# Reordering the first loads, transposes and copies of a fused convolution and two-layer MLP kernel

## The chip, the cores and the metric

The kernel runs on one core of a Trainium2 chip. The metric is device time in microseconds (us) for one execution. One profiled execution of each kernel gives the trace; other executions give a time and a mean granted TensorE clock (the share of its full clock that TensorE was allowed, 1 is full).

PE is TensorE, PEld its weight loads, ACT is ScalarE, DVE is VectorE, POOL is GpSimd, SP is SyncE. L837 means line 837 of that kernel's source.

## The reference, cut to what matters

```python
# x (8, 4096, 192), weight (8 heads, 7 taps): a causal convolution per head, softmaxed taps
w = softmax(weight, axis=-1)
out = np.einsum('hk,bskhg->bshg', w, windows_of(x))      # 6 zeros ahead of each sequence
# then 32768 tokens through w_in (192, 2048) and w_out (2048, 192)
h = out.reshape(-1, 192) @ w_in
g = np.where(h > 0, h, exp(min(h, 0)) - 1)                # ELU
return g @ w_out                                          # float32
```

## The kernel before

Tokens are worked off in 32 "supers" of 1024. In a super there are 16 blocks of 128 hidden columns, and in a block two units (one for each half of the tokens). So there are 1024 units. One unit goes through four engines:

- PE: three matmuls `H <- att, w_in` (64 rows, 512 columns) into one PSUM bank;
- ACT: `E <- exp(H)`;
- POOL: `E <- min(E, 1)`;
- DVE: `gT <- max(E - 1, H)`, after which the PSUM bank is free. I count units by these gT operations.

PE then multiplies gT by w_out into accumulator banks. The convolution of super 0 is done in a special way, so that work can begin early: x is cast, transposed on PE and convolved by matmuls with diagonal tap matrices (a tap is one of the 7 weights of the filter). The halo, `xh` and `xbh` in the code, is the 8 rows of x just before the second half of the tokens; it is cast and transposed apart. The convolutions of later supers take four groups of matmuls with a banded matrix `Tm`; ACT evicts each group (`csb`), and one transposing DMA makes `att` of it. For super 1 these groups stand at the blocks of `EARLY_CONV`.

All of w_in sits twice in SBUF, in partitions 0 to 63 for one unit of a block and 64 to 127 for the other. It is loaded to the lower half through POOL's DMA queue in three parts (blocks 0 to 3, 4 to 7, 8 to 15). The upper half is a copy: parts 0 and 1 by DVE, the third by a DMA that SP issues once it has landed. The parts that the change and the argument touch:

```python
WARM, FILL = (6, 1, 4), 1
WCOLS = ((0, 4 * FC), (4 * FC, 8 * FC), (8 * FC, 16 * FC))
EARLY_CONV = (6, 7, 9, 10)
# ...
start_up = [("t", j) for j in (3, 0, 1, 2)] + [("d", j) for j in range(3)]   # 3: halo
for what in start_up:
    pe_order.append(what)
    if what[0] == "t" and what[1] < 3:
        pe_order.append(("w", 0, FILL))          # a zero matmul, 128x512
# ... POOL: one queue, in this order
load_w_in(0); load_w_in(1); load_w_out(0)        # w_out(0): blocks 0 to 7
load_x(1, 0); load_x(1, 1)
load_w_in(2); load_w_out(1)
load_x(2, 0); load_x(2, 1)
# ... ACT at the start
W(s_xh, 16); activation(xbh <- xh, Copy)         # halo cast
W(s_xs, 16)
for j in range(3): activation(xb[j] <- xs[j], Copy)
# ... SP
# band matrix out to DRAM, wait, Tm back in; then
W(s_w[2], 48)
sy.dma_start(w_in[HP:P, :, c0:c1], w_in[0:HP, :, c0:c1]).then_inc(s_wd, 16)
# ... PE, first matmul of a unit in block q, upper half (r == 1)
W(s_w[part], 48)
if r == 1 and part < 2: W(s_wc, part + 1)
elif r == 1:            W(s_wd, 16)
```

Of the kernel before, what the change touches and what calls it, by code (L numbers as in the profile page):

```python
# [6 lines left out]
ACT = mybir.ActivationFunctionType  # L7
# [28 lines left out]
CONV_AT = (14, 18, 23, 25)  # L36
QB = 2
WARM = (6, 1, 4)
FILL = 1
WCOLS = ((0, 4 * FC), (4 * FC, 8 * FC), (8 * FC, 16 * FC))  # L40
HALO = 8
BW = P + CW
XI = SUP // P
# [3 lines left out]
E_DVE = ()  # L47
HELD = {"h": 2900.0, "c": 1300.0, "a": 1400.0}

EARLY_CONV = (6, 7, 9, 10)  # L50
EARLY_O = (4, 8)
PACE0, UNTIL = 1160.0, 24
X_AT = ((2, 1, 1), (1, 1, 0))
# [3 lines left out]
def bass_lightweight_conv__then__act_elu_kernel(  # L57
# [15 lines left out]
    NQ = FF // FC  # L73
# [12 lines left out]
    pe_order, plan = [], []  # L86
# [100 lines left out]
    for s in range(1, NS):  # L187
        for u in range(CU):
            at = NQ * (s - 2) + CONV_AT[u] if s > 1 else EARLY_CONV[u]
            conv_steps.setdefault(at, []).append(CU * s + u)  # L190


    start_up = [("t", j) for j in (3, 0, 1, 2)] + [("d", j) for j in range(3)]
    for i, (b, what) in enumerate(
        ((0, ("t", 0)), (3, ("t", 3)), (1, ("t", 1)), (2, ("t", 2)))
        + ((4, ("d", 0)), (5, ("d", 1)), (6, ("d", 2)), (7, ("d", 2)))
# [19 lines left out]
    for second in range(2):  # L216
        for rt in range(2):
            g = rt ^ second
            k, b = divmod(NP - O_AT[g], NB)
# [17 lines left out]
    pe_order += [("w", 0, WARM[0]), ("s",), ("w", 0, WARM[2])]  # L237
    for what in start_up:
        pe_order.append(what)
        if what[0] == "t" and what[1] < 3:  # L240
            pe_order.append(("w", 0, FILL))
    pe_order += [item for _, item in sorted(plan, key=lambda p: p[0])]
    turn_at = {}
    dve_order, evacs, unit_at_conv = [], [], {}
    for at, item in sorted(plan, key=lambda p: p[0]):
# [8 lines left out]
        elif item[0] == "o" and item[-1]:  # L254
            turn_at[item[1:3]] = turn_at.get(item[1:3], 0) + 1
            if turn_at[item[1:3]] == visits[item[1:3]]:
                what = ("e",) + item[1:3]
# [25 lines left out]
    with ExitStack() as stack:  # L283
# [6 lines left out]
        def sema(name):  # L290
            return stack.enter_context(nc.semaphore(name))
# [8 lines left out]
        xh = sbuf("xh", [HALO, D], FP32)  # L300
        xbh = sbuf("xbh", [HALO, 3, 2, HP], BF16)
# [22 lines left out]
        H = psum("H", [P, NBANK, GS])  # L324

        s_wq = sema("s_wq")
        s_w = [sema(f"s_w{i}") for i in range(5)]
        s_wc = sema("s_wc")
        s_sel = sema("s_sel")
        s_set = sema("s_set")  # L330
# [5 lines left out]
        s_xh = sema("s_xh")  # L336
        s_wb = sema("s_wb")
        s_xz = sema("s_xz")
        s_cast = sema("s_cast")
        s_tap = sema("s_tap")  # L340
# [47 lines left out]
        def att_need(s):  # L388
# [1 line left out]


        first_read = {
            ("t", 0): (0, 2),
            ("t", 1): (1, 0),
            ("t", 2): (2, 0),
            ("t", 3): (0, 1),
            ("d", 0): (3, 0),
            ("d", 1): (0, 3),
            ("d", 2): (4, 4),
# [69 lines left out]
        @block.gpsimd  # L469
        def _gpsimd(g: bass.BassGpSimd):  # L470
            W = Waits(g)

            def load_x(s, gr):
                b = s % NXB
                if s >= NXB:
                    W(s_cv, CU * (s - NXB))
                if s == NXB:
                    W(s_zw, 1)
                def windows(w0, w1, rows):
                    src = bass.AP(  # L480
                        tensor=x_flat.tensor,
                        offset=(s * SUP + gr * GS + w0 * CW - PAD) * D,
                        ap=[[D, rows], [CW * D, w1 - w0], [1, D]],
                    )
                    g.dma_start(  # L485
                        xg[0:rows, b, 2 * w0 + gr : 2 * w1 : 2, :], src
                    ).then_inc(s_x[b][gr], 16)

                if s == NS - 1 and gr == 1:
                    windows(0, NWIN - 1, P)  # L490
                    windows(NWIN - 1, NWIN, GS - CW * (NWIN - 1) + PAD)
                else:
                    windows(0, NWIN, P)

            def batch_zeros(s):

                W(s_x[s % NXB][0], x_need[s, 0])
                g.memset(xg[0:PAD, s % NXB, 0, :], 0.0).then_inc(s_z)

            def load_w_in(k):  # L500
                c0, c1 = WCOLS[k]
                for j in range(3):
                    g.dma_start(  # L503
                        w_in[0:HP, j, c0:c1],
                        bass.AP(
                            tensor=moe_w_in.tensor,
                            offset=8 * j * FF + c0,
                            ap=[[CPH * FF, HEADS], [FF, 8], [1, c1 - c0]],
                        ),
                    ).then_inc(s_w[k], 16)  # L510

            def load_w_out(k):
                q = slice(NQ // 2 * k, NQ // 2 * (k + 1))
                g.dma_start(
                    w_out[:, q, :], moe_w_out.rearrange("(q p) d -> p q d", p=FC)[:, q, :]
                ).then_inc(s_w[3 + k], 16)

            g.memset(ones[:], 1.0).then_inc(s_id)
            W(s_id, 1)
            g.affine_select(  # L520
                out=ident[:],
                in_=ones[:],
                pattern=[[-1, P]],
                compare_op=ALU.is_equal,
                fill=0.0,
                base=0,
                channel_multiplier=1,
            ).then_inc(s_id)
            for step in range(2):
                W(s_id, 2 + step)  # L530
                g.affine_select(
                    out=owner[:, :],
                    in_=owner[:, :] if step else ones[0:HEADS, :],
                    pattern=[[0, 2], [1 - 2 * step, HP]],
                    compare_op=ALU.is_ge,
                    fill=0.0,
                    base=7 * step,
                    channel_multiplier=8 * (2 * step - 1),
                ).then_inc(s_id)
            W(s_id, 4)  # L540
            g.affine_select(
                out=block8[:, :, :],
                in_=ones[0:HEADS, 0 : HEADS * KSIZE].rearrange("p (h k) -> p h k", h=HEADS),
                pattern=[[1, HEADS], [0, KSIZE]],
                compare_op=ALU.is_equal,
                fill=0.0,
                base=0,
                channel_multiplier=-1,
            ).then_inc(s_id)
            load_w_in(0)  # L550
            load_w_in(1)
            load_w_out(0)
            for gr in range(2):
                load_x(1, gr)
            load_w_in(2)
            load_w_out(1)
            for gr in range(2):
                load_x(2, gr)
            for i, (n, u) in enumerate(units):
                s, at_n = divmod(i // 2, NQ)  # L560
                if i % 2 == 0 and at_n == ZERO_AT and (s + 2) % SPB == 0 and s + 2 < NS:
                    batch_zeros(s + 2)
                for to_load in x_before.get(i, ()):
                    load_x(*to_load)
                W(s_exp, i + 1)
                g.tensor_scalar(  # L566
                    out=E[:, i % NE, :],
                    in0=E[:, i % NE, :],
                    scalar1=1.0,
                    scalar2=0.0,  # L570
                    op0=ALU.min,
                    op1=ALU.max,
                ).then_inc(s_clp)

        @block.scalar
        def _scalar(a):
            W = Waits(a)
# [5 lines left out]
            a.activation(scr[:, 1:2], scr[:, 0:1], ACT.Exp)  # L583
            W(s_set, 2)
            a.activation(wex[:], wq2[:], ACT.Exp).then_inc(s_wex)
            W(s_xh, 16)
            a.activation(  # L587
                xbh[:, :, 1, :].rearrange("p j (h e) -> p j h e", e=8),
                xh[:, :].rearrange("p (h j e) -> p j h e", j=3, e=8),
                ACT.Copy,  # L590
            ).then_inc(s_cast)
            W(s_xs, 16)
            for j in range(3):
                a.activation(  # L594
# [12 lines left out]
            for item in act_order:  # L607
# [4 lines left out]
                elif item[0] == "h":  # L612
                    i = unit_at[item[1:]]
# [10 lines left out]
        def _vector(v):  # L624
            W = Waits(v)

            def upper_half(v, k):
                c0, c1 = WCOLS[k]
                W(s_w[k], 48)
                v.tensor_copy(w_in[HP:P, :, c0:c1], w_in[0:HP, :, c0:c1]).then_inc(s_wc)  # L630
# [39 lines left out]
                H[:, bank_of["d", 2], 0:KSIZE].unsqueeze(2).to_broadcast([P, KSIZE, P]),  # L670
                ALU.mult,
            ).then_inc(s_tap)
            v.tensor_copy(
                wband[:, :, P - KSIZE : P][:, :, ::-1],
                H[:, bank_of["d", 2], HP : HP + HEADS * KSIZE].rearrange(
                    "p (h k) -> p h k", h=HEADS
                ),
            ).then_inc(s_tap)
            for at, j in enumerate((3, 0)):
                W(s_xt, at + 1)  # L680
                v.tensor_copy(*transposed(j)).then_inc(s_fd)
            upper_half(v, 0)
            W(s_first, 2)
            v.tensor_copy(*first_att(1, 0, GS)).then_inc(s_fd)  # L684
            W(s_first, 3)
            v.tensor_copy(*first_att(2, GS // 2, GS)).then_inc(s_fd)
            upper_half(v, 1)
            for item in dve_order:
                if item[0] == "e":
                    v.tensor_copy(*out_evac(W, *item[1:])).then_inc(s_od)  # L690
# [2 lines left out]
                i = unit_at[n, u]  # L693
                s, q = divmod(n, NQ)
# [14 lines left out]
        def _tensor(pe):  # L709
            W = Waits(pe)  # L710
# [15 lines left out]
            for item in pe_order:  # L726
# [25 lines left out]
                elif item[0] == "t":  # L752
                    j = item[1]
                    W(s_id, 2)
                    if j < 3:
                        W(s_cast, j + 2)
                        for i in range(XI):
                            for g in range(2):
                                rows = slice(HP * g, HP * (g + 1))
# [6 lines left out]
                                    tile_position=(HP * g, HP * g),  # L766
                                )
                    else:
                        W(s_xz, 1)
                        W(s_cast, 1)  # L770
                        for jj in range(3):
                            ins = pe.matmul(
                                H[:, bank_of[item], HALO * jj : HALO * (jj + 1)],
# [5 lines left out]
                    ins.then_inc(s_xt)  # L779
                elif item[0] == "d":  # L780
                    j = item[1]
                    W(s_tap, 2)
                    first_evacuated(W, ("t", j))
                    first_evacuated(W, ("t", 3))
                    for tap in range(KSIZE):
# [61 lines left out]
                else:  # L847
# [6 lines left out]
                        wait_bank(("a", k, g))  # L854
                    if visit is not None and not opens:
                        W(s_turn[g], turns[k, g])
                    W(s_w[3 + q // (NQ // 2)], 16)
                    W(s_tt, tt_count(NQ * t + q, g))
                    t0 = 2 * P * half + P * kb
                    ins = pe.matmul(  # L860
# [80 lines left out]
```

## Time and profile before

| What | Value |
|---|---|
| time, first three runs | 730.87 us median (730.77 to 732.73) |
| span of the profiled run | 730.1 us (its time 732.09 us, mean granted clock 0.994) |
| PE busy | 721.1 us, 99% |
| period of 32 units once it runs evenly (units 128 to 1000) | 21.87 us |
| gT unit 0 / 16 / 36 starts | 16.09 / 29.09 / 43.70 us |

From the page of the profiled run, the busy table's row of all engines and the row of the granted clock (40 slices of 18 us, 9 is full):

```profile
PE 721.1 (99%) x11856; PEld 682.7 (93%) x11857; DVE 640.7 (88%) x1042; ACT 677.3 (93%) x1287; POOL 669.2 (92%) x1114
...
PEclk9899999999999999999999999999999999999999
```

PE is full nearly everywhere; only the second slice has a clock below full. The change can only matter at the start. Here is the chain of waits of the kernel before (start, duration, what), around 24 us:

```profile
23.94 0.34 PE H L860 x2
24.28 2.02 issue
26.30 0.34 PE H L837
```

PE stands still for 2.02 us. "Issue" says that the profile names no releaser; the timeline of SP's DMA issues (start, us, engine, line, what) gives it:

```profile
10.59 0.36 SPq L892 DMA_DIRECT2D Tm<-conv_band  x1
20.67 0.72 SPq L899 DMA_DIRECT2D w_in<-w_in  x1
```

The upper copy of the third part of w_in is issued at 20.67, right after that part has landed (20.65), and lands at 26.20. PE's first matmul of block 8's upper half is what waits. The windows view (busy time and, in brackets, instructions of each engine; then granted clock, DMA share, GB/s) shows what follows:

```profile
core 0: us, PE busy (x) PEld busy (x) DVE busy (x) ACT busy (x) POOL busy (x), PEclk, DMA share, GB/s
18.58:25.41 6.83, 4.38 (x45) 2.30 (x40) 6.59 (x11) 5.55 (x12) 5.97 (x11) 1.00 1.26 185
25.41:32.24 6.83, 5.94 (x43) 4.57 (x45) 3.00 (x6) 2.71 (x6) 2.70 (x5) 0.50 0.01 4
```

For 6.83 us TensorE gets half its clock, from 25.41 on, when PE had stood still for 1.13 us. The timeline of DVE, in which each line merges successive gT operations, shows the pace of units: 0.60 us each, then gaps.

```profile
16.09 7.86 DVE L699 SCALAR_TENSOR_TENSOR gT<-E,H 128x512 f16<-128x512 f32 x13 [1.17 <-POOL E L566]
24.19 1.29 DVE L699 SCALAR_TENSOR_TENSOR gT<-E,H 128x512 f16<-128x512 f32 x2 [0.23 <-POOL E L566]
25.73 0.69 DVE L699 SCALAR_TENSOR_TENSOR gT<-E,H 128x512 f16<-128x512 f32 x1 [0.26 <-POOL E L566]
29.09 1.28 DVE L699 SCALAR_TENSOR_TENSOR gT<-E,H 128x512 f16<-128x512 f32 x2 [2.67 <-POOL E L566]
```

Last, the start-up on PE (timeline): halo transpose, x transposes with zero matmuls between, convolution at 9.00.

```profile
6.00 0.21 PE L772 MATMUL H<-ident,xbh 8*128 8x8 bf16 x3 [0.33 <-ACT xbh L587]
6.43 0.63 PE L760 MATMUL H<-ident,xb 64*64 64x64 bf16 x16 [0.22 <-ACT xb L594]
7.00 0.39 PE L734 MATMUL H<-zw 128*128 128x512 bf16 x1
...
9.00 4.74 PE L788 MATMUL H<-xT,taps 128*128 128x512 bf16 x28 [0.16 <-issue]
```

### The profile page before, as it was taken

The numbers are of one execution on the slowest core, as the hardware profiler recorded it, in microseconds if no ns is written. First come the engines' busy times: TensorE is split into PE (matmuls) and PEld (weight loads), VectorE is DVE, ScalarE is ACT, GpSimd is POOL, SyncE is SP. The second block draws the span as 40 slices with busy tenths as digits, with TensorE's granted clock in tenths as the row PEclk, the third lists the DMA queues.
The fourth block names the chain that finished last, engine by engine and source line by source line (L and its number), as shares of the span: only waits on it lengthen the run. The fifth ranks groups of instructions, "written<-read, shape, count | busy, mean of one in ns | idle before, by whom it ended". The sixth has DMA issues, their size and how long they took to land.

```text
span 730.1 us, 27614 instructions
## 1 busy us (share of the span) xinstructions
PE 721.1 (99%) x11856; PEld 682.7 (93%) x11857; DVE 640.7 (88%) x1042; ACT 677.3 (93%) x1287; POOL 669.2 (92%) x1114
## 2 busy tenths in 40 slices
PE   8899999999999999999999999999999999999998
PEld 3579999999999999999999999999999999999997
DVE  4799898889898889899889898889998889998993
ACT  5799999999999999999999999999999999999993
POOL 8699999999999999999999999999999999999892
PEclk9899999999999999999999999999999999999999
DMA  9634546543535644635543545643535543644212
GB/s 185 96 54 70 86 81 86 97 61 72 89 79 86 96 66 67 90 78 85 97 64 69 90 78 86 96 68 66 93 75 85 95 67 67 95 74 84 70 34 67
DMA packets 132699, 59.21 MB, mean 81 GB/s; under 512 B 98648, under 2 KB 131808, under 8 KB 132576
## 3 DMA queue, kind: packets, MB, share of 16 engines
q1 hardware_dynamic: 88144, 39.66, 23.7%
q0 software_dynamic: 44016, 16.79, 22.8%
q8 instruction: 93, 1.52, 0.8%
q10 hardware_dynamic: 416, 0.98, 0.4%
q14 instruction: 30, 0.25, 0.1%
HBM read 34.83 MB, written 25.66 MB: 83 GB/s over the span
## 4 chain that ended last, share of the span: by engine, by line
PE 95%; POOL 2%; ACT 1%; DVE 1%; DMA 1%; issue 0%; SPq 0%; DVEq 0%
PE H L860 53%; PE H L837 37%; PE H L810 3%; POOL E L566 1%; DVE gT L699 1%; PE H L788 1%; ACT E L615 1%; DMA xh<-in_x_dram 1%; POOL xg L485 0%; PE H L760 0%; ACT csb L611 0%; ACT osb L619 0%; PE H L734 0%; DVE osb L690 0%; ACT xb L594 0%
## 5 line engine op out<-in xcount | busy, mean ns | idle before, releaser
L699 DVE SCALAR_TENSOR_TENSOR gT<-E,H 128x512 f16<-128x512 f32 x1024 | 633.2, 683 | 70.5 <-POOL E L566 69.1
L837 PE MATMUL H<-att,w_in 64*128 64x512 bf16 x3072 | 684.0, 378 | 2.6 <-issue 2.0
L860 PE MATMUL H<-w_out,gT 64*128 64x192 f16 x8192 | 686.2, 243 | 0.2
L566 POOL TENSOR_SCALAR E<-E 128x512 f32<-128x512 f32 x1024 | 606.6, 612 | 47.6 <-ACT E L615 36.1
L860 PEld LDWEIGHTS H<-w_out,gT 64*128 64x128 f16 x8192 | 629.2, 94 | 21.1 <-PE H L860 2.3
L615 ACT ACTIVATE E<-H 128x512 f32<-128x512 f32 x1024 | 593.9, 601 | 33.4 <-PE H L837 7.6
L837 PEld LDWEIGHTS H<-att,w_in 64*128 64x128 bf16 x3072 | 275.5, 93 | 9.3 <-issue 3.1
L810 PE MATMUL H<-xg,Tm 64*112 64x240 bf16 x496 | 93.4, 268 | 0.9 <-DVE gT L699 0.9
L611 ACT ACTIVATE csb<-H 112x480 bf16<-112x480 f32 x124 | 69.8, 563 | 0.0
L619 ACT ACTIVATE osb<-H 128x384 f32<-128x384 f32 x127 | 61.7, 486 | 7.5 <-PE H L860 7.4
L810 PEld LDWEIGHTS H<-xg,Tm 64*112 64x112 bf16 x496 | 58.0, 127 | 4.9 <-issue 1.8
L485 POOL DMA_DIRECT2D xg<-in_x_dram x63 | 56.2, 894 | 0.2 <-issue 0.2
L690 DVE COPY osb<-H 128x384 f32<-128x384 f32 x1 | 0.6, 559 | 8.5 <-PE H L860 8.5
L734 PE MATMUL H<-zw 128*128 128x512 bf16 x15 | 6.0, 503 | 1.2 <-DVE zw L632 1.2
L734 PEld LDWEIGHTS H<-zw 128*128 128x128 bf16 x16 | 1.7, 117 | 4.2 <-issue 2.5
L503 POOL DMA_DIRECT2D w_in<-in_moe_w_in_dram x9 | 5.3, 613 | 0.0
L788 PE MATMUL H<-xT,taps 128*128 128x512 bf16 (+1 forms) x28 | 4.7, 326 | 0.2 <-issue 0.2
L788 PEld LDWEIGHTS H<-xT,taps 128*128 128x128 bf16 x28 | 2.7, 97 | 1.9
L606 ACT ACTIVATE att<-H 128x512 bf16<-128x512 f32 (+1 forms) x2 | 1.0, 490 | 3.7 <-PE H L788 3.7
L684 DVE CAST att<-H 128x512 bf16<-128x512 f32 x1 | 0.7, 693 | 3.7 <-PE H L788 3.7
L587 ACT ACTIVATE xbh<-xh 8x192 bf16<-8x192 f32 x1 | 0.4, 362 | 2.4 <-DMA xh<-in_x_dram 2.4
L581 ACT ACT_TABLE_LOAD x1 | 1.3, 1283 | 1.2 <-PEq L926 1.2
(38 smaller groups left out, 19.6 us busy)
## 6 DMA issues: line engine op xcount, KB each, us to landing
out_dram<-osb SPq DMA_DIRECT2D x127, 192.0 KB, 3.4
xg<-in_x_dram POOLq DMA_DIRECT2D x61, 240.0 KB, 5.0
xs<-in_x_dram ACTq DMA_DIRECT2D x1, 768.0 KB, 4.6
w_out<-in_moe_w_out_dram POOLq DMA_DIRECT2D x2, 384.0 KB, 10.8
att<-csb SPq DMA_TRANSPOSE x31, 4.6
conv_band<-wband SPq DMA_DIRECT2D x1, 480.0 KB, 4.8
Tm<-conv_band SPq DMA_DIRECT2D x1, 448.0 KB, 8.0
w_in<-in_moe_w_in_dram POOLq DMA_DIRECT2D x6, 64.0 KB, 3.0
```

What stands on the lines that cost most here:

```text
L485: g.dma_start(xg[0:rows, b, 2 * w0 + gr : 2 * w1 : 2, :], src).then_inc(s_x[b][gr], 16)
L503: g.dma_start(w_in[0:HP, j, c0:c1], bass.AP(tensor=moe_w_in.tensor, offset=8 * j * FF + c0, ap=[[CPH * FF, HEADS], [FF, 8], [1, c1 - c0]], ...
L566: g.tensor_scalar(out=E[:, i % NE, :], in0=E[:, i % NE, :], scalar1=1.0, scalar2=0.0, op0=ALU.min, op1=ALU.max,).then_inc(s_clp)
L611: a.activation(*conv_evac(W, m), ACT.Copy).then_inc(s_ce)
L615: a.activation(E[:, i % NE, :], H[:, bank_of[item], :], ACT.Exp).then_inc(s_exp)
L619: a.activation(*out_evac(W, *item[1:]), ACT.Copy).then_inc(s_oev[item[2]])
L699: v.scalar_tensor_tensor(out=gT[:, s % NG3, q, u, :], in0=E[:, i % NE, :], scalar=1.0, in1=H[:, bank_of[item], :], op0=ALU.subtract, op1=A ...
L734: pe.matmul(H[:, bank, :], zw[:, 0:P], zw[:, 0:GS], start=True, stop=True)
L788: ins = pe.matmul(H[:, bank_of[item] + part, c0:c1], taps[:, tap, :], xT[:, j, HALO - PAD + tap + c0 : HALO - PAD + tap + c1], start=(tap ...
L810: ins = pe.matmul(H[0:CW, bank_of["c", m], 256 * q : 256 * q + UC], Tm[rows, h, 0:CW], xg[rows, s % NXB, :, CPH * h : CPH * (h + 1)].rearr ...
L837: ins = pe.matmul(H[:, bank_of[item[:3]], :], w_in[HP * r : HP * (r + 1), j, FC * q : FC * (q + 1)], att[HP * r : HP * (r + 1), s % 2, j, ...
L860: ins = pe.matmul(acc_of(k, g)[:, D * kb : D * (kb + 1)], gT[HP * rt : HP * (rt + 1), t % NG3, q, g, t0 : t0 + P], w_out[HP * rt : HP * (r ...
```

## The change

Its intent is to end both losses. The third part of w_in is queued straight behind the second; w_out comes in three parts (blocks 0 to 3, 4 to 7, 8 to 15) around x of super 1; super 1's convolutions stand at blocks 7 to 10. At the start, the first x transpose goes ahead of the halo, no zero matmuls stand between, the halo is cast by DVE, and DVE copies both upper parts of w_in in a row.

```diff
--- before.py
+++ after.py
@@ -36,8 +36,8 @@
 CONV_AT = (14, 18, 23, 25)
 QB = 2
 WARM = (6, 1, 4)
-FILL = 1
 WCOLS = ((0, 4 * FC), (4 * FC, 8 * FC), (8 * FC, 16 * FC))
+WOUT = (0, 4, 8, 16)
 HALO = 8
 BW = P + CW
 XI = SUP // P
@@ -47,7 +47,7 @@
 E_DVE = ()
 HELD = {"h": 2900.0, "c": 1300.0, "a": 1400.0}
 
-EARLY_CONV = (6, 7, 9, 10)
+EARLY_CONV = (7, 8, 9, 10)
 EARLY_O = (4, 8)
 PACE0, UNTIL = 1160.0, 24
 X_AT = ((2, 1, 1), (1, 1, 0))
@@ -190,7 +190,7 @@
             conv_steps.setdefault(at, []).append(CU * s + u)
 
 
-    start_up = [("t", j) for j in (3, 0, 1, 2)] + [("d", j) for j in range(3)]
+    start_up = [("t", j) for j in (0, 3, 1, 2)] + [("d", j) for j in range(3)]
     for i, (b, what) in enumerate(
         ((0, ("t", 0)), (3, ("t", 3)), (1, ("t", 1)), (2, ("t", 2)))
         + ((4, ("d", 0)), (5, ("d", 1)), (6, ("d", 2)), (7, ("d", 2)))
@@ -237,8 +237,6 @@
     pe_order += [("w", 0, WARM[0]), ("s",), ("w", 0, WARM[2])]
     for what in start_up:
         pe_order.append(what)
-        if what[0] == "t" and what[1] < 3:
-            pe_order.append(("w", 0, FILL))
     pe_order += [item for _, item in sorted(plan, key=lambda p: p[0])]
     turn_at = {}
     dve_order, evacs, unit_at_conv = [], [], {}
# ... (one more semaphore; the order of two waits renumbered) ...
@@ -510,7 +508,7 @@
                     ).then_inc(s_w[k], 16)
 
             def load_w_out(k):
-                q = slice(NQ // 2 * k, NQ // 2 * (k + 1))
+                q = slice(WOUT[k], WOUT[k + 1])
                 g.dma_start(
                     w_out[:, q, :], moe_w_out.rearrange("(q p) d -> p q d", p=FC)[:, q, :]
                 ).then_inc(s_w[3 + k], 16)
@@ -549,11 +547,12 @@
             ).then_inc(s_id)
             load_w_in(0)
             load_w_in(1)
+            load_w_in(2)
             load_w_out(0)
             for gr in range(2):
                 load_x(1, gr)
-            load_w_in(2)
             load_w_out(1)
+            load_w_out(2)
             for gr in range(2):
                 load_x(2, gr)
             for i, (n, u) in enumerate(units):
@@ -583,12 +582,6 @@
             a.activation(scr[:, 1:2], scr[:, 0:1], ACT.Exp)
             W(s_set, 2)
             a.activation(wex[:], wq2[:], ACT.Exp).then_inc(s_wex)
-            W(s_xh, 16)
-            a.activation(
-                xbh[:, :, 1, :].rearrange("p j (h e) -> p j h e", e=8),
-                xh[:, :].rearrange("p (h j e) -> p j h e", j=3, e=8),
-                ACT.Copy,
-            ).then_inc(s_cast)
             W(s_xs, 16)
             for j in range(3):
                 a.activation(
@@ -670,21 +663,27 @@
                 H[:, bank_of["d", 2], 0:KSIZE].unsqueeze(2).to_broadcast([P, KSIZE, P]),
                 ALU.mult,
             ).then_inc(s_tap)
+            W(s_xh, 16)
+            W(s_xz, 1)
+            v.tensor_copy(
+                xbh[:, :, 1, :].rearrange("p j (h e) -> p j h e", e=8),
+                xh[:, :].rearrange("p (h j e) -> p j h e", j=3, e=8),
+            ).then_inc(s_xz)
             v.tensor_copy(
                 wband[:, :, P - KSIZE : P][:, :, ::-1],
                 H[:, bank_of["d", 2], HP : HP + HEADS * KSIZE].rearrange(
                     "p (h k) -> p h k", h=HEADS
                 ),
             ).then_inc(s_tap)
-            for at, j in enumerate((3, 0)):
+            for at, j in enumerate((0, 3)):
                 W(s_xt, at + 1)
                 v.tensor_copy(*transposed(j)).then_inc(s_fd)
             upper_half(v, 0)
+            upper_half(v, 1)
             W(s_first, 2)
             v.tensor_copy(*first_att(1, 0, GS)).then_inc(s_fd)
             W(s_first, 3)
             v.tensor_copy(*first_att(2, GS // 2, GS)).then_inc(s_fd)
-            upper_half(v, 1)
             for item in dve_order:
                 if item[0] == "e":
                     v.tensor_copy(*out_evac(W, *item[1:])).then_inc(s_od)
@@ -753,7 +752,7 @@
                     j = item[1]
                     W(s_id, 2)
                     if j < 3:
-                        W(s_cast, j + 2)
+                        W(s_cast, j + 1)
                         for i in range(XI):
                             for g in range(2):
                                 rows = slice(HP * g, HP * (g + 1))
@@ -766,8 +765,7 @@
                                     tile_position=(HP * g, HP * g),
                                 )
                     else:
-                        W(s_xz, 1)
-                        W(s_cast, 1)
+                        W(s_xz, 2)
                         for jj in range(3):
                             ins = pe.matmul(
                                 H[:, bank_of[item], HALO * jj : HALO * (jj + 1)],
@@ -779,7 +777,7 @@
                     ins.then_inc(s_xt)
                 elif item[0] == "d":
                     j = item[1]
-                    W(s_tap, 2)
+                    W(s_tap, 2 if j == 2 else 1)
                     first_evacuated(W, ("t", j))
                     first_evacuated(W, ("t", 3))
                     for tap in range(KSIZE):
@@ -854,7 +852,7 @@
                         wait_bank(("a", k, g))
                     if visit is not None and not opens:
                         W(s_turn[g], turns[k, g])
-                    W(s_w[3 + q // (NQ // 2)], 16)
+                    W(s_w[2 + next(k for k in range(1, 4) if q < WOUT[k])], 16)
                     W(s_tt, tt_count(NQ * t + q, g))
                     t0 = 2 * P * half + P * kb
                     ins = pe.matmul(
```

## The prediction

> **What bounds the kernel now.** TensorE (PE) is busy 99% of the span (busy table) and holds 95% of the chain of waits. From about 45 us on it runs back to back: in the timeline the gT operations of VectorE repeat every 21.87 us per 1024 rows (unit 96 at 85.09 us, unit 128 at 106.97). The change does not touch that part; only the first 45 us can move.

> There the trace shows two losses.
> 1. Start-up. xs has landed at 5.38 us, but ScalarE first casts the halo (0.36 us from 5.50, waiting for xh), so x casts begin at 5.77. Three filler matmuls stand between the transposes (0.32 us each in the chain), and the start-up convolution begins at 9.00.
> 2. The third part of w_in. Its load stands behind half of w_out and x of super 1 in one queue and lands at 20.65 us; the copy to the upper partitions is issued at 20.67 and lands at 26.20. PE stands still from 24.28 to 26.30 ("issue 2.02" in the chain). Then the granted clock is 0.50 from 25.41 to 32.24 (windows view), and 64x512 matmuls take 0.63 instead of 0.38 us. [...] Together: gT unit 16 starts at 29.09 us, though units 0 to 12 came every 0.60 us from 16.09 (extrapolated: 25.7); by unit 36 (43.70 us, against 37.7) 6.0 us are lost. Units 21 to 36 came at VectorE's pace of 0.6 us, so nothing is made up.

> **What changes, costed.**
> - Halo cast off ScalarE: x casts about 0.3 us earlier. On VectorE it costs about 0.3 us where there is slack.
> - No fillers, back to back: convolution starts at about 8.1 us (estimate: cast 0.53, three transposes of 0.56 to 0.63, halo 0.2). Gain 0.9 us, on the chain.
> - w_in part 3 directly behind part 2 (landed 10.02 us): I expect landing at 13 to 15 us, the upper copy at 18 to 20.5, needed at about 23. The 2.0 us stall goes, and with it the half-clock stretch (6.8 us, about 3.4 us of work).
> - w_out part 1 (landed 15.26) moves to about 15 to 16, needed at about 17; x of super 1 (19.59) to 18 to 20, needed at 21 to 22 as its convolution moves one block later. I expect no new stall over 0.5 us.
> - Convolutions now in four consecutive blocks: ScalarE has about 1.45 us a block there (two exponentials of 0.49, one csb eviction of 0.46) against VectorE's 1.21, so 0.5 to 1 us comes back.

> **Sum.** 0.9 + 6.0 - 0.5 to 1: about 5.6 us less, all on the critical path, as later work is PE-bound. Predicted 725.3 us, range 723.6 to 728.2. Chances: faster by over 2% 0.01, within 2% 0.98, slower by over 2% 0.01.

> **What would show it.** Convolution starting near 8.1 and gT unit 0 near 15.2; no PE idle of 2 us near 24; clock 1.00 from 5 us to the end of the program; gT unit 36 at 37 to 38.5 and unit 128 at 101 to 102 us; period still 21.87.

> **What would make it wrong.** A new wait for w_out part 1, x of super 1 or Tm in the shared queue; a half-clock stretch anyway[...]; the unprofiled runs of before not having the half-clock stretch at all, which would leave only 1 to 3 us to gain.

As written, 0.9 + 6.0 - 0.5 to 1 comes to 5.9 to 6.4 us, of which the prediction makes "about 5.6" and takes it off 730.87. That the half-clock stretch goes with the stall was the author's estimate from one trace, in which the half clock began 1.13 us into the stall of 2.02 us. The 0.3 us of the halo cast on VectorE was an estimate too; in the changed kernel's trace the cast took 0.27 us, against 0.36 on ScalarE before.

## More of the kernel before

A mean of runs is a mean of all executions of that kernel in a group of experiments.

The change moves lines, so L837, L860, L810, L699, L615, L611 and L566 of the kernel before are L835, L858, L808, L698, L608, L604 and L565 of the changed one.

A static plan fixes the order of PE's instructions and the PSUM bank of every item.

## The result, and the profile after

| | before | changed |
|---|---|---|
| first comparison, median | 731.42 us (730.77 to 732.73, 4 runs) | 727.35 us (726.73 to 727.61, 4 runs) |
| ratio, first comparison | | 0.9941 (95%: 0.9924 to 0.9958) |
| ratio, repeated (after_again, 5 runs against 9) | | 0.9940 (0.9927 to 0.9952) |
| span of the profiled run | 730.1 us | 725.5 us |
| gT unit 0 / 16 / 36 starts | 16.09 / 29.09 / 43.70 us | 14.82 / 25.11 / 39.17 us |

A ratio is the mean time of one kernel's fast runs over the mean of the other's fast runs of the same rounds, so it is not quite the ratio of the medians quoted. The change gains about 4.3 us, 0.6%, clear of noise. It lies in the predicted range, at 2 us more than the predicted value.

Where the time went is seen in the trace: from unit 24 on, the two kernels run in parallel, 4.5 us apart (unit 24: 36.22 and 31.70; unit 128: 106.97 and 102.43; unit 1000: 703.02 and 698.39). All of it is decided in the first 32 us. Unit 36 (39.17) and unit 128 (102.43) come later than the forecasts of 37 to 38.5 and 101 to 102 us. The changed kernel's start-up on PE (timeline):

```profile
5.98 0.63 PE L759 MATMUL H<-ident,xb 64*64 64x64 bf16 x16
6.55 0.23 PE L770 MATMUL H<-ident,xbh 8*128 8x8 bf16 x3
6.71 1.08 PE L759 MATMUL H<-ident,xb 64*64 64x64 bf16 x32
7.72 4.75 PE L786 MATMUL H<-xT,taps 128*128 128x512 bf16 x28
```

The convolution starts 1.28 us earlier, and so does unit 0. The same two windows have the full clock now:

```profile
18.58:25.41 6.83, 4.67 (x55) 2.95 (x53) 6.19 (x11) 5.26 (x11) 5.50 (x10) 1.00 1.25 186
25.41:32.24 6.83, 6.25 (x80) 4.05 (x78) 5.49 (x9) 6.11 (x12) 5.43 (x10) 1.00 0.37 68
```

But a wait is left. SP's issues and the chain of waits of the changed kernel:

```profile
11.16 0.36 SPq L890 DMA_DIRECT2D Tm<-conv_band  x1
14.72 0.72 SPq L897 DMA_DIRECT2D w_in<-w_in  x1
```

```profile
14.72 8.14 DMA w_in<-w_in
22.86 0.09 issue
22.95 0.31 PE H L835
```

The copy is issued 6 us earlier than before, yet takes 8.14 us instead of 5.5, and PE waits 1.19 us for it. Its first packet ran only at 19.00, 4.28 us after the issue (in the kernel before at 22.12, 1.45 us after it). In DVE's timeline, unit 16 comes late, and the units after it come at 0.96 us instead of 0.60:

```profile
14.82 9.65 DVE L698 SCALAR_TENSOR_TENSOR gT<-E,H 128x512 f16<-128x512 f32 x16 [1.89 <-POOL E L565]
25.11 0.69 DVE L698 SCALAR_TENSOR_TENSOR gT<-E,H 128x512 f16<-128x512 f32 x1 [0.64 <-POOL E L565]
26.06 0.69 DVE L698 SCALAR_TENSOR_TENSOR gT<-E,H 128x512 f16<-128x512 f32 x1 [0.26 <-POOL E L565]
```

ACT's timeline of the changed kernel shows what else holds these units up (conv_banks and tiny_evict test it). In blocks 8 to 10 ACT has two exponentials and one csb eviction a block, and then waits for PE, which waits for the eviction:

```profile
23.79 0.60 ACT L608 ACTIVATE E<-H 128x512 f32<-128x512 f32 x1 [0.87 <-PE H L835]
24.28 0.56 ACT L604 ACTIVATE csb<-H 112x480 bf16<-112x480 f32 x1
24.73 0.60 ACT L608 ACTIVATE E<-H 128x512 f32<-128x512 f32 x1
25.71 0.60 ACT L608 ACTIVATE E<-H 128x512 f32<-128x512 f32 x1 [0.38 <-PE H L835]
26.20 0.56 ACT L604 ACTIVATE csb<-H 112x480 bf16<-112x480 f32 x1
```

### The profile page after: what moved, and what is told of

It reads as the page before. It is cut to its first block, busy times and chain, and to the rows that moved or that the text cites. A ratio compares the mean times of both kernels' runs of the same rounds, so it can differ in the third digit from the quotient of the medians.

```text
span 725.5 us, 27613 instructions
## 1 busy us (share of the span) xinstructions
PE 717.7 (99%) x11854; PEld 679.9 (94%) x11854; DVE 640.6 (88%) x1043; ACT 676.8 (93%) x1286; POOL 669.7 (92%) x1115
## 4 chain that ended last, share of the span: by engine, by line
PE 93%; POOL 2%; DMA 2%; ACT 1%; DVE 0%; issue 0%; DVEq 0%; POOLq 0%
PE H L858 53%; PE H L835 37%; PE H L808 3%; POOL E L565 1%; DMA w_in<-w_in 1%; DMA w_in<-in_moe_w_in_dram 1%; ACT E L608 1%; POOL w_in L501 1%; ACT csb L604 0%; POOL xg L483 0%; ACT osb L612 0%; DVE gT L698 0%; POOL owner L529 0%; DVE osb L689 0%; POOL block L539 0%
## 5 line engine op out<-in xcount | busy, mean ns | idle before, releaser
L587 ACT ACTIVATE xb<-xs 128x512 bf16<-128x512 f32 x3 | 1.7, 619 | 2.2 <-DMA xs<-in_x_dram 2.2
L623 DVE COPY w_in<-w_in 64x1536 bf16<-64x1536 bf16 x2 | 1.6, 800 | 2.4 <-DMA w_in<-in_moe_w_in_dram 2.4
L512 POOL DMA_DIRECT2D w_out<-in_moe_w_out_dram x3 | 2.7, 951 | 0.0
```

## The experiments

Starts of gT units in the profiled run of each kernel (from the trace, us). "Lost" is unit 36's start, less unit 0's start, less 36 times 0.60: what is lost against an undisturbed pace.

```
                unit 0  unit 15  unit 16  unit 22  unit 36   lost
before           16.09    25.73    29.09    35.03    43.70    6.0
start_only       14.83    24.47    29.66    35.05    43.72    7.3
warm_stall       16.25    25.89    28.96    33.40    42.08    4.2
queue_only       17.79    27.43    28.04    32.49    41.16    1.8
changed          14.82    23.80    25.11    30.51    39.17    2.8
after_again      15.01    23.99    24.59    29.86    38.53    1.9
after_old_conv   15.10    24.74    25.34    29.80    38.47    1.8
copy_first       15.21    27.06    28.09    34.04    42.71    5.9
conv_banks       15.09    24.06    24.76    30.38    39.06    2.4
w_in_split       15.24    24.21    24.81    30.09    38.76    1.9
split_banks      14.79    23.76    24.46    30.09    38.77    2.4
tiny_evict       14.85    23.82    24.42    28.68    37.37    0.9
split_spread2    14.92    23.90    24.50    28.87    37.90    1.4
split_spread3    14.93    24.03    24.63    28.37    38.62    2.1
```

The kernel before was executed beside every group of experiments. These 31 executions fall into two groups by clock: 11 with a mean granted clock of 0.999 or 1.000, at 729.72 to 730.57 us (mean 730.13), and 20 with 0.994 to 0.998, at 731.50 to 733.49 us (mean 732.32). The half-clock stretch of the trace is thus not in every run of it. Nor is it as long in all 20: a mean of 0.994 or 0.995, as in the traced execution, for six of them (mean 732.67 us), 0.997 or 0.998 for fourteen (mean 732.17), which fits a stretch of about 3.4 us (my estimate: 3.4 us at half clock are 0.0023 of 730 us, and the end of the program adds up to 0.001). The nine runs of the changed kernel all have 0.999 or more, at 726.73 to 728.32 us (mean 727.42).

### queue_only: the queue order alone

```diff
 # kernel before, with
+WOUT = (0, 4, 8, 16)
-load_w_in(0); load_w_in(1); load_w_out(0); load_x(1, ..); load_w_in(2); load_w_out(1)
+load_w_in(0); load_w_in(1); load_w_in(2); load_w_out(0); load_x(1, ..); load_w_out(1); load_w_out(2)
```

> The kernel before, with only the queue order changed (third part of w_in ahead, w_out in three parts). Theory (the two parts are not additive: the stall on the upper copy of w_in decides when the convolution-era work can go on): the copy lands near 22.9 us instead of 26.2, the wait before it shrinks from 2.0 us to 0 to 0.7 us because PE arrives there 1.3 us later than in the changed kernel, no half-clock stretch; so about 3 us less than before (about 728). Rival (parts add up, the queue is worth only the 2 us stall): about 2 us less, with a half-clock stretch remaining.

Measured: 728.71 us mean of six, ratio 0.9958 (0.9937 to 0.9979). Three runs took 727.68 to 727.98 us and three 729.55 to 729.60. The traced run is one of the slow ones, and its start-up transposes took 1.06 instead of 0.63 us, as the full clock came only at 10.3 us, against 4.93 in before and 5.47 in the changed kernel (the other two slow runs were not traced):

```profile
6.50 1.06 PE L762 MATMUL H<-ident,xb 64*64 64x64 bf16 x16
...
10.47 0.39 PE L736 MATMUL H<-zw 128*128 128x512 bf16 x1
```

Here PE never waits for the copy (landed at 21.11), and the loss is 1.8 us instead of 6.0. The three fast runs are 2.3 us under the full-clock runs of before. So the queue order is most of the gain: 2.3 us, against 2.7 for the whole change, both against full-clock runs. The missing half clock and, roughly, the time are as the theory said, the copy came earlier than its 22.9; the rival's remaining half-clock stretch was not there.

### start_only: the start-up part alone

```diff
 # kernel before, with start_up (0, 3, 1, 2), no FILL, halo cast on DVE, upper copies in a row;
 # queue order, w_out in two parts and EARLY_CONV = (6, 7, 9, 10) as before
```

> The kernel before, with only the start-up part (order of transposes, no fillers, halo cast on VectorE, upper copies in a row). Theory: the convolution starts at 7.7 us, gT unit 0 at 14.8, but PE then stands about 3.3 us for the copy that still lands at 26.2 us; gT unit 36 and the time are unchanged (within 0.5 us of before). Rival (a start-up gain is kept to the end): 1.3 us less than before.

Measured: 732.20 us mean, ratio 1.0008 (0.9990 to 1.0026); nothing gained. Unit 0 comes 1.26 us earlier, unit 36 at 43.72 against 43.70. The chain of waits shows where it went:

```profile
22.70 0.32 PE H L856 x2
23.02 3.84 issue
```

The wait for the copy, which lands at 26.77 (26.20 in before), grew from 2.02 to 3.84 us. All six runs had a clock of 0.995 to 0.998. The theory holds: alone, a faster start only reaches the same wait earlier.

### warm_stall: the wait filled with zero matmuls

```diff
 # kernel before
+if n == 8 and r == 1 and j == 0:
+    wait_bank(item[:3])
+    for _ in range(9):
+        pe.matmul(H[:, bank, :], zw[:, 0:P], zw[:, 0:GS], start=True, stop=True)
```

> The kernel before, with nine 128x512 zero matmuls (about 1.9 us at full clock) put where PE stands before the third part of w_in, so that the wait is filled and its length is the same. Separates the wait from the half clock that follows. Theory (the half clock costs as much as or more than the wait itself): no half-clock stretch, gT unit 16 still near 29, but units 16 to 21 come faster, and 1.5 to 3 us less in all. Rival (ScalarE's convolution evictions, not the clock, pace units 16 to 21): the clock stays full but the time stays within 0.7 us of before.

Measured: 731.18 us mean, ratio 0.9994 (0.9976 to 1.0012), all six runs at a clock of 0.999 or 1.000. PE's timeline shows the filled wait:

```profile
24.37 2.12 PE L828 MATMUL H<-zw 128*128 128x512 bf16 x9
26.79 0.37 PE L847 MATMUL H<-att,w_in 64*128 64x512 bf16 x1 [0.30 <-DMA w_in<-w_in]
```

In this pair of traces the wait ends at about the same time (26.79 and 26.30), unit 16 comes at 28.96 against 29.09, and units 16 to 22 then take 4.44 us instead of 5.94. So the half clock, for its full 6.83 us, costs 1.5 us in the traces. By the means, this kernel is 1.1 us under the half-clock runs of before, but 1.1 us over its full-clock runs. The theory's size of 1.5 to 3 us is met, at its lower end, only by the pair of traces; against all eleven runs of before beside it the difference of the means is 0.4 us, which is within the rival's 0.7. Why the full-clock runs of before are faster still is open: none of them was traced, so it is not known whether their copy landed earlier.

### after_old_conv: convolutions at the old blocks

```diff
 # changed kernel
-EARLY_CONV = (7, 8, 9, 10)
+EARLY_CONV = (6, 7, 9, 10)
```

> The changed kernel, with the convolutions of super 1 at blocks 6, 7, 9 and 10 again. x of super 1 lands at 20.2 us and PE would want it at about 19.2: theory: about 1 us of wait for x there, which then also brings the wait for the upper copy forward; in exchange the evictions on ScalarE are spread, so units 16 to 21 come at under 0.9 us each; net within 0.7 us of the changed kernel. Rival (four convolutions in a row cost 2 us that the old spacing does not): 1 us or more faster than the changed kernel.

Measured: 728.46 us mean, ratio 0.9957 (0.9934 to 0.9980), in two groups again: three runs at 726.99 to 727.23 us with full clock, three at 728.77 to 730.99 us with 0.994 to 0.997. With full clock it is as fast as the changed kernel. The expected 1 us of waiting for x is not in its (full-clock) trace, where x landed at 19.04 us. What the half-clock runs waited for was not traced. The later blocks may buy that no run loses its clock (three of six lose it here, none of nine there); but queue_only has the old blocks too and kept its clock in six of six, so this is not shown.

### copy_first: the upper copy issued ahead of Tm

```diff
 # changed kernel, SP
 # band out
+W(s_w[2], 48); sy.dma_start(w_in upper <- lower)
 W(s_band, 16); sy.dma_start(Tm <- band)
-W(s_w[2], 48); sy.dma_start(w_in upper <- lower)
```

> The changed kernel, with SyncE issuing the upper copy of w_in before the load of Tm. In the changed kernel the copy is issued at 14.72 us and its first packet runs at 19.0. Theory A (it waits at the DMA engines while the 384-byte packets of the gpsimd queue, x of super 1 above all, go first): still issued at 14.7, first packet still near 19, landing 21.5 to 23, and Tm lands with or after it; time the same or up to 2 us slower, as Tm is late for the convolution. Theory B (it waits behind Tm in SyncE's own queue): first packet near 15 to 16, landing near 18 to 19, no PE wait for the copy.

Measured: 730.64 us mean, ratio 0.9992 (0.9967 to 1.0017). SP's issues, and PE's waits (who waited for what: us in all, times, longest):

```profile
14.84 0.71 SPq L891 DMA_DIRECT2D w_in<-w_in  x1
15.60 0.59 SPq L893 DMA_DIRECT2D Tm<-conv_band  x1
```

```profile
PE H L808 <- DMA Tm<-conv_band: 2.2, 1, 2.2
```

Nothing stood ahead of the copy in SP's own queue, and still its first packet ran at 19.08 us, 4.2 us after the issue, as in the changed kernel (4.3). Tm, issued at 15.60, had its first packet at 20.64. Theory B falls: the copy does not wait behind Tm in SP's own queue. Theory A is right about the first packets, but the time is 3.2 us over the changed kernel's mean, more than its 2 us: PE now waits 2.2 us for Tm, and three of the four runs have a clock of 0.995 to 0.998. Packets finished in each half microsecond of the changed kernel show what the DMA engines did meanwhile (from the trace's packet records; some rows left out):

```
from    POOL queue, 384 B    SP queue: Tm    SP queue: copy
14.5           235                  0               0
15.0           189                 10               0
16.0            44                 41               0
17.0           171                 10               0
18.0           234                  0               0
18.5           249                  0               0
19.0           136                  0              37
20.0            60                  0              59
```

First w_out and x run alone, then SP's Tm makes up most of the bytes, then w_out and x run alone again, then the copy gets its turn. Of the POOL queue's 384-byte packets, 1,433 finished between the copy's issue and its first packet, about 90 for each of 16 engines. That the engines were taken does not explain the length: in before, start_only and warm_stall POOL's queue was as busy when the copy was issued, at about 21 us, and the first packet came after 1.42 to 1.45 us and 38 to 45 such packets for each engine. What makes it 1.4 or 4.3 us stays open.

### conv_banks: separate PSUM banks for super 1's convolutions

```diff
 # changed kernel, the plan
-freed[bank_of["c", m]] = clock[1] + MM_C + HELD["c"]
+freed[bank_of["c", m]] = clock[1] + MM_C + HELD["c"] + (2500 if m < 2 * CU else 0)
```

> The changed kernel, with the plan holding the PSUM banks of super 1's convolutions 2.5 us longer, so that the four convolutions take four different banks (in the changed kernel the last three share one, each waiting for the csb eviction of the one before). Theory (this chain PE, ScalarE E, ScalarE csb, PE paces gT units 16 to 21 at 0.96 us): units 16 to 21 come at 0.6 to 0.8 us, 1 to 2 us less than the changed kernel. Rival (ScalarE is simply full there, 1.45 us a block): 0.73 us a unit at best and under 1 us gained, or nothing since another bank wait takes its place.

Measured: 727.82 us mean, ratio 0.9956 (0.9941 to 0.9972); not faster than the changed kernel. Units 16 to 21 took 4.90 us against 4.79. The theory falls: with four different banks PE waits instead for gT of an earlier unit to free a bank, as the chain of waits shows there (PE, ACT exponential, ACT eviction, ACT exponential, POOL, DVE, PE). Taking the shared bank away gains nothing, as another wait for a bank takes its place: the rival's second case.

### w_in_split: parts of 4, 8 and 4 blocks

```diff
 # changed kernel
-WCOLS = ((0, 4 * FC), (4 * FC, 8 * FC), (8 * FC, 16 * FC))
+WCOLS = ((0, 4 * FC), (4 * FC, 12 * FC), (12 * FC, 16 * FC))
 # DVE: upper_half(v, 1) moved behind the evictions of the first att
```

> The changed kernel, with parts of w_in of 4, 8 and 4 blocks instead of 4, 4 and 8: VectorE copies the upper half of the second part (1.4 us, in its idle 1.9 us before gT unit 0), and the DMA copy on SyncE's queue is wanted only at block 12. Theory: the 1.2 us wait of PE at 22.9 goes; units 16 to 21 keep their 0.96 us chain, so 1.0 to 1.3 us less than the changed kernel, if VectorE's copy ends before 14.8. Rival (the wait is hidden by the chain that follows): under 0.4 us.

Measured: 727.15 us mean of six (727.06 to 727.30), ratio 0.9947 (0.9932 to 0.9962). The wait for the copy is gone (unit 16 comes 0.60 us after unit 15), but the time is only 0.3 us under the mean of the changed kernel. The expected 1.0 to 1.3 us were too much, because the wait of 1.19 us in the changed kernel's trace is not in all of its runs: in after_again the copy landed at 22.20 and PE did not wait for it. Its six runs lie within 0.24 us; but three other kernels with this edit spread over 0.52 to 0.81 us (split_banks, split_spread2, split_spread3), so an even time is not shown to come of it.

### split_banks: both

```diff
 # w_in_split and conv_banks together
```

> The two edits together (w_in parts of 4, 8, 4; separate banks for super 1's convolutions). Theory: both waits are on the chain, one after the other, so the gains add: 2 to 3 us less than the changed kernel, about 724.5 to 725.5. Rival (they cover each other, both delaying the same units): no better than the better one of the two.

Measured: 727.62 us mean, ratio 0.9954 (0.9939 to 0.9969). It gains nothing on either. The theory of adding gains falls, as each had fallen alone.

### after_again: the changed kernel once more

```diff
 # no edit
```

> The changed kernel, unchanged, for more executions beside the kernel before. The runs of before so far fall in two groups: 11 of 22 at 729.7 to 730.5 us with a granted clock of 0.999 or more, 11 at 731.5 to 733.5 with 0.994 to 0.998. Theory (part of the gain is that the changed kernel is never re-throttled): all runs of the changed kernel at 0.999 or more and within 726.5 to 728; about 2.9 us under the full-clock runs of before and about 5 under the others. Rival (its four runs only happened to miss the half clock): one or more of the six at 0.998 or less and 2 us longer.

Measured: 727.49 us median (727.10 to 728.32, 5 runs), clock 0.999 or 1.000 in all; ratio 0.9940 (0.9927 to 0.9952). One run, 728.32 us, is a little over the expected 728. The changed kernel stays at full clock in nine runs of nine.

### tiny_evict: convolution evictions of super 1 cut short (wrong result)

```diff
 # w_in_split
+v.memset(csb[:, 1, :], 0.0)                          # DVE, while idle
+if m < 2 * CU: to, frm = to[:, :, 0:1, :], frm[:, :, 0:1, :]
 a.activation(to, frm, ACT.Copy).then_inc(s_ce)
```

> Wrong result on purpose: the version with w_in in parts of 4, 8 and 4 blocks, with the four csb evictions of super 1 on ScalarE cut to 16 columns (the rest of that csb half is zeroed by VectorE while it is idle). Theory (ScalarE's 0.47 us eviction on top of two exponentials is what delays blocks 7 to 10): units 15 to 22 come in under 5.0 us instead of 5.9, and up to 1 us less in all. Rival (PSUM banks and PE's order pace them): 5.5 us or more.

Measured: relative error 0.17, as meant; 725.81 us mean, ratio 0.9916 (0.9901 to 0.9932). ACT's timeline:

```profile
22.98 0.60 ACT L611 ACTIVATE E<-H 128x512 f32<-128x512 f32 x1 [0.41 <-PE H L839]
23.47 0.18 ACT L607 ACTIVATE csb<-H 112x16 bf16<-112x16 f32 x1
23.62 0.60 ACT L611 ACTIVATE E<-H 128x512 f32<-128x512 f32 x1
24.51 0.60 ACT L611 ACTIVATE E<-H 128x512 f32<-128x512 f32 x1 [0.29 <-PE H L839]
```

Units 15 to 22 take 4.86 us instead of 5.88, and the whole takes 1.3 us less than w_in_split (in the two traces 1.0 of it here, and 0.4 as unit 0 started earlier). So the time that ACT spends on four evictions is on the chain. About 0.7 us of these seven units (4.86 less 7 times 0.60) remains without it.

### split_spread2 and split_spread3: convolutions further apart

```diff
 # w_in_split
-EARLY_CONV = (7, 8, 9, 10)
+EARLY_CONV = (7, 8, 10, 11)      # split_spread2
+EARLY_CONV = (7, 9, 11, 12)      # split_spread3
```

> The version with w_in in parts of 4, 8 and 4 blocks, and super 1's convolutions at blocks 7, 8, 10 and 11. Theory (each convolution costs ScalarE about 0.47 us which a block without one gives back only at 0.2 us): 0.2 to 0.6 us less than the same with 7, 8, 9, 10 (727.15), unless the transpose then comes late for unit 32. Rival: no difference.

> The same with the convolutions at blocks 7, 9, 11 and 12. Theory: 0.3 to 0.8 us less than with 7, 8, 9, 10 if the transpose of super 1 lands before unit 32 wants it at about 34.5 us; it is issued about 2.6 us later than at 28.4 and takes about 4, so it lands near 35 and gives some or all of it back. Rival: as fast as with 7, 8, 9, 10 or slower.

Measured: split_spread2 726.72 us median (726.51 to 727.03, mean 726.75), ratio 0.9929 (0.9916 to 0.9941); split_spread3 727.61 us (727.16 to 727.97), ratio 0.9939. The first gains 0.4 us on w_in_split; every one of its five runs is faster than every run of the changed kernel in the same rounds (727.10 to 728.32). It is the fastest correct version here. In split_spread3, units up to 22 come earlier still (28.37), but the transpose of super 1 lands at 33.99, and PE waits for it before unit 32 (PE's waits):

```profile
PE H L835 <- DMA att<-csb: 0.6, 1, 0.6
```

Unit 32 starts at 36.22 there, at 35.51 in split_spread2: the gain is given back, as the expectation had allowed.

## Why the prediction was right, and where its sum was off

The predicted 725.3 us lies 2 us below the measured 727.35, inside the range. The predicted gain was 5.6 us, the measured one 4.1 (medians) to 4.5 (traces). Of the 2 us, 1.2 lie in the base: the 5.6 us were worked out from the trace of an execution that took 732.09 us, one of the half-clock group, but were taken off 730.87, the median of three others. The rest, about 0.9 us, is the sum's own error, and it is small partly by luck. The terms as written, 0.9 + 6.0 - 0.5 to 1, give 5.9 to 6.4 us and not 5.6 (the prediction does not say why it takes less), and a start that gained more than forecast (1.27 against 0.9 us) hides part of a loss that was forecast too small.

1. *Only the first 45 us can move.* Right: the period stayed 21.87 us, and the kernels run in parallel from unit 24 on.
2. *Start-up 0.9 us.* Unit 0 came 1.27 us earlier (convolution at 7.72, not 8.1). But the prediction called it "on the chain", which holds only together with the queue order: start_only gains nothing. Added to the queue order, start-up and later convolutions bring about 0.4 us (727.42 against 727.84, the mean of the three faster runs of queue_only; the ranges overlap).
3. *The 2.0 us stall goes; the copy lands at 18 to 20.5.* The load landed at 14.70, as said (13 to 15). The copy took 8.1 us, not 5.5, as 4.3 us passed before its first packet instead of 1.45. In the trace 1.19 us of PE's wait remained; in another execution of the same kernel none.
4. *The half-clock stretch goes.* Right in all nine runs. Its size was wrong: the prediction counted 3.4 us of lost PE work, but units 16 to 22 lost only 1.5 us by it in the pair of traces (warm_stall); that ACT's evictions held those units up too is the likely reason, not shown. And half clock is in 20 of 31 executions of before only, which the prediction listed among the things that could make it wrong. Against the full-clock runs of before the gain is 2.7 us, against the others 4.9.
5. *Convolutions in a row give back 0.5 to 1 us.* This is the term that was most undersized. The loss to unit 36 is 2.8 us in the changed kernel and 1.9 us in its repetition, where PE never waits for the copy; of that, 1.0 us goes when ACT's evictions are cut (0.9 left in tiny_evict against 1.9 in w_in_split). But that the convolutions stand in a row is not what costs: at the old blocks and without a wait for the copy the loss is 1.8 us as well (queue_only, after_old_conv). So it was inside the 6.0 us all along: of these, 1.8 go with the half clock when the stall is filled (4.2 left in warm_stall), and 1.8 are left when there is no stall at all (queue_only). By the way "lost" is counted, 1.27 (start) + 6.0 (lost before) - 2.8 (lost now) = 4.5 us.

So the mechanism held: the load moved ahead takes away the stall and the half clock. The step that failed is the subtraction "6.0 - 0.5 to 1". It put all 6.0 us down to the stall and the half clock, but 1.9 to 2.8 us, not 0.5 to 1, were still lost without them.

## What to carry to other kernels

When a wait is taken out, ask what else would hold up the same instructions once it is gone: some of the loss before it may belong to that other work, and stays. Two small changes at the start are not a sum: an earlier start is worth nothing if the next thing that PE needs lands at a fixed time (start_only: unit 0 1.26 us earlier, nothing gained). A copy issued earlier need not run as much earlier: issued 5.95 us earlier, its first packet ran 3.1 us earlier here, and the shared DMA engines finished 1,433 packets of another queue between its issue and that packet. A smaller last part, wanted later, with idle VectorE copying the rest, took PE's wait away (w_in_split: unit 16 0.60 us after unit 15, against 1.31 in the changed kernel's trace). And before a predicted gain is taken off a median, look whether the traced execution belongs to the same group as that median.
